# When the first gated weights are converted: behind the first attention results instead of ahead of them

## The chip, the cores and the metric

The kernel runs on one core of a Trainium2 chip. Its time is the device time of one execution in microseconds (us). Before the change three runs were timed; the median was 837.14 us, the lowest 832.61, the highest 839.86.

The engines work side by side, each in its own fixed order of instructions: TensorE (PE) multiplies, VectorE (DVE) and ScalarE (ACT) work on tiles, GpSimd (POOL) does a little and issues some transfers, SyncE (SP) issues most transfers. They wait for each other by semaphores. Matmul results land in PSUM, everything else is in SBUF or in DRAM.

## The reference

Three parts, one behind the other, all in fp32:

```python
scores = scale * q @ k.T;  scores = cap * tanh(scores / cap)        # 4 batches x 12 heads, 448 x 64
attn = softmax(scores) @ v                                          # scale = 1/8, cap = 30
x = attn, heads side by side                                        # 1792 tokens x 768
a, b = x @ w1, x @ w2;  h = (a * b) @ w3 @ w_out                    # 768 -> 1024 -> 1024 -> 768
h = h @ w_in                                                        # 768 -> 1024
solu = h * softmax(h);  ln = layer norm of solu, times g_ln
out = ln @ w_out2                                                   # 1024 -> 768
```

## The kernel before

**Arithmetic.** Each fp32 operand is split into a high and a low part that TensorE multiplies exactly, and a product is the sum of three matmuls (low times high, high times low, high times high; `THREE` lists which parts). The high part is a cast on ScalarE (L174), the low part a subtraction on VectorE (L175). Weights that come as fp32 words in a packed form are first brought into a work tile `cv` by three rows on VectorE (L168, L169, L170).

**Stages.** Attention runs over 24 pairs of heads (o12 is pair 12), each in four chunks (sc13_2 is the scores of chunk 2 of pair 13; p, hi and lo are its exponentials and their two parts; o13_0 and o13_1 its results, which ScalarE copies out of PSUM, L306). Beside it, with matmuls put between those of attention by `fill`, goes a second stream, `beside`: first the *fold*, which multiplies the weights w_out, w3 and w_in into one matrix, then the *gated* products x·w1 and x·w2 (L607). The fold has two stages: stage 1 makes the blocks w34 and stores them in DRAM (576 matmuls, L378), stage 2 loads them again, splits them, and multiplies by w_in (288 matmuls, L396, sixteen tiles f2_f_nh of eighteen each). `load34` has one block on its way while another is used. Behind attention come seven products for the second factor (L769), the layer norm and the last product.

**What sets the order.** `Ahead` holds a list of conversions that are taken strictly in turn, a few in each turn of the attention loop. An item has a load on SP into one of three landing tiles `ld`, a first step on VectorE, and a rest. The function given last with an item is its gate: while it says no, the item isn't loaded, nor is anything behind it. `pos[0]` counts the fold's matmuls as they are written, `STAGE1` is 576 and `HALFWAY` 144, so that `STAGE1 + HALFWAY` is the middle of stage 2.

The items that matter here: `plan_w(f)` converts block f of the gated weights in three items (512 KB loaded for each) into the tile wt*f*; wt0 and wt1 are the first two, wt0 is read first by the first gated matmul. `plan_x(b)` makes batch b's tokens xs from the attention results xr, in three parts; `free_x` is its gate. The numbers in ld40 or cv47 count the items of the list. In `gated`, each of the first six wt tiles is stored in DRAM for a second pass once the program comes to L618. `plan_last` scales the last weights by g_ln into one of two tiles wg (L539), which is stored in wg_dr (L540).

From these calls a scheduler makes each engine's order, so a change in the list can move rows on all engines.

Of the kernel before, what the change touches and what calls it, by code (L numbers as in the profile page):

```python
# [25 lines left out]
NC, NF = DM // P, DF // P  # L26
# [14 lines left out]
PASSES = ((0, 1), (2, 3))  # L41
# [4 lines left out]
def raw(ap):  # L46

    return ap.bitcast(F32)
# [50 lines left out]
def attention_moe_solu(ctx: ExitStack, tc: tile.TileContext, q, k, v, cap, w12, w3t, wo, win, wout2, g_ln, out):  # L99
# [50 lines left out]
    def landing(i, src, n, kind):  # L150
        t = conv.tile([P, 2 * HALF], U32, tag="ld", bufs=LANDS, name=f"ld{i}")
        lands[i] = t[:, :n].bitcast(kind)
        dst = lands[i]
        if len(src.shape) == 3:
            dst = dst.rearrange("p (a b) -> p a b", a=src.shape[1])
        elif len(src.shape) == 4:
            dst = dst.rearrange("p (a b c) -> p a b c", a=src.shape[1], b=src.shape[2])
            for g in range(src.shape[1]):
                sync.dma_start(out=dst[:, g], in_=src[:, g])
            return  # L160
        loads[i] = sync.dma_start(out=dst, in_=src)

    def convert(i, n):

        d = lands.pop(i).rearrange("p (n w) -> p n w", w=2)
        lo, hi = d[:, :, 0], d[:, :, 1]
        x = conv.tile([P, HALF], U32, tag="cv", bufs=2, name=f"cv{i}")[:, :n]
        dve.tensor_scalar(x, hi, 5, 2, ALU.logical_shift_left, ALU.logical_shift_right)  # L168
        dve.scalar_tensor_tensor(x, hi, 0xC0000000, x, ALU.bitwise_and, ALU.bitwise_or)  # L169
        dve.scalar_tensor_tensor(x, lo, 29, x, ALU.logical_shift_right, ALU.bitwise_or)  # L170
        cvs[i] = x.bitcast(F32)

    def split(th, tl, x):
        act.copy(th, x)  # L174
        dve.tensor_tensor(tl, x, raw(th), ALU.subtract)  # L175

    def plan64(key, src, n, dst, gate=None, there=None):

        i = len(ahead.items)

        def rest():
            th, tl = dst()
            split(th, tl, cvs.pop(i))
        ahead.add(key, lambda: landing(i, src.bitcast(U32), 2 * n, U32), lambda: convert(i, n), rest, gate, there)
# [139 lines left out]
    fw, pos, place, held = {}, [0], {}, {}  # L324
# [30 lines left out]
    STAGE1, HALFWAY = NQ * NC * NF * 3, NC * NF * 3  # L355
# [50 lines left out]
    wt, xs, rb, fin = {}, {}, {}, set()  # L406
# [5 lines left out]
    def slot12(f, i):  # L412
        if i == 0:
            p = place["wt"] if f >= NF and (f - NF) % 3 == 2 else res[0]
            wt[f] = p.tile([P, 2, 2 * DM], F32R, tag="wres", bufs=1 if p is not res[0] else 2, name=f"wt{f}")
        return wt[f][:, 0, i * HALF:(i + 1) * HALF], wt[f][:, 1, i * HALF:(i + 1) * HALF]

    def free12(f):

        if f == NF + 2:  # L420
            return "wt" in place
        before = f - 2 if f < NF + 2 else f - 3
        return pos[0] >= STAGE1 and (f < 2 or (before, PASSES[before // NF][-1]) in fin)

    def plan_w(f):
        for i in range(3):
            plan64(("w", f, i), w12[f, i], HALF, lambda i=i: slot12(f, i), lambda: free12(f))

    def plan_again(f):
        def load():  # L430
            for i in range(3):
                slot12(f, i)
            sync.dma_start(out=raw(wt[f]), in_=w12_dr[block(f)])
        for i in range(3):
            ahead.add(("w", f, i), load if i == 0 else (lambda: None), lambda: None, lambda: None, None, lambda: free12(f))

    def place_x(b, c):

        n = b * NC + c
        if n < W3 or n >= 2 * W3:  # L440
            return w3p.tile([P, 2, HALF], F32R, tag="w3", bufs=W3, name=f"xs{b}_{c}")[:, :, :S]
        return place["x"].tile([P, 2, S], F32R, tag="xs", bufs=W3, name=f"xs{b}_{c}")

    def free_x(b, part):
        if (b, part) not in stored:
            return False
        if b == 0:
            return pos[0] >= STAGE1 + (HALFWAY if part else 0)
        return (pos[0] >= STAGE1 + HALFWAY if (b, part) == (1, 0) else "x" in place) and (b < 3 or (NF - 1, 0) in fin)

    def plan_x(b, parts=range(NPAIR // 2)):
        for part in parts:
            if (b, part) == (B - 1, NPAIR // 2 - 1):

                plan_again(NF + 2)
            i = len(ahead.items)
            pairs = slice(2 * part, 2 * part + 2)

            def load(i=i, pairs=pairs):
                rb[i] = conv.tile([P, 2, S], F32, tag="rb", name=f"rb{i}")  # L460
                for j in range(2):
                    row = r_dr[b].rearrange("(n j) s -> j n s", j=2)[j:j + 1, pairs]
                    pool.dma_start(out=rb[i][j * D:(j + 1) * D], in_=row.to_broadcast([D, 2, S]))

            def first(i=i, part=part):

                for c in (2 * part, 2 * part + 1):
                    xs[b, c] = place_x(b, c)
                one = raw(xs[b, 2 * part + 1][:, 0, :1])
                pool.memset(one, 1.0)  # L470
                dve.scalar_tensor_tensor(xr[b, part], xr[b, part], one, rb.pop(i), ALU.mult, ALU.mult)

            def rest(part=part):
                x = xr.pop((b, part))
                for i in range(2):
                    split(xs[b, 2 * part + i][:, 0], xs[b, 2 * part + i][:, 1], x[:, i])
            ahead.add(("x", b, part), load, first, rest, None, lambda part=part: free_x(b, part))
# [55 lines left out]
    def plan_last(f):  # L533
        for u in range(2):
# [5 lines left out]
                sync.dma_start(out=wg_dr[f, u], in_=t)  # L540
            ahead.add(("g", f, u), lambda i=i, u=u: landing(i, wout2[f, u].bitcast(U32), DM, U32), lambda i=i: convert(i, DM // 2), rest)

    plan_w(0)
    plan_x(0)
    plan_w(1)
    plan_x(1)
    for f in range(2, NF):
# [419 lines left out]
```

## Time and profile before

| | before |
|---|---|
| runs | 837.14 us median (832.61, 837.14, 839.86) |
| the profiled execution's own time | 834.68 us |
| its span, first to last instruction | 832.9 us |
| mean granted TensorE clock | 0.998 |
| TensorE (PE) busy | 820.4 us, 98% |
| VectorE (DVE) busy | 586.8 us, 70% |
| ScalarE (ACT) busy | 478.8 us, 57% |
| GpSimd (POOL) busy | 75.8 us, 9% |
| moved by DMA | 167.19 MB, mean 201 GB/s |

Busy is the time in which an engine worked on an instruction, and the share is of the span. The granted clock is 1.00 where TensorE ran at 2.4 GHz all the time and 0.50 where at 1.2 GHz. Times in the rows further down count from the span's start.

### The profile page before, as it was taken

To read this page: it belongs to the slowest core of one execution; us is meant where nothing else is said; L and a number is where in the kernel's file an instruction comes from. 1 tells how busy PE (TensorE), PEld (TensorE's weight loads), DVE (VectorE), ACT (ScalarE), POOL (GpSimd) and SP (SyncE) were. 2 spreads that over 40 slices of the span, in tenths; PEclk is the share of its full clock that TensorE was granted. 3 is DMA by queue.
4 is the path that set the end of the run, shared out by engine and by line. 5 is a ranking of instruction groups with operands and counts; after the bars stand their busy time and mean duration, and the time that the engine had idled before them with its cause. 6 is when DMAs were issued, how large, how long until landed. Compare 5 with 4: busy or idle time off the path is not lost.

```text
span 832.9 us, 12192 instructions
## 1 busy us (share of the span) xinstructions
PE 820.4 (98%) x4363; PEld 683.6 (82%) x4363; DVE 586.8 (70%) x1048; ACT 478.8 (57%) x739; POOL 75.8 (9%) x149
## 2 busy tenths in 40 slices
PE   8999999999999999999989999999999999999998
PEld 4657888876777888888869999998888888999997
DVE  5989969788866797788826744332988876994452
ACT  6767868778777876777642301112565555863341
POOL 1110010110311211111111000000000000000000
PEclk9999999999999999999999999999999999999999
DMA  7888645568976465689537999972533326834211
GB/s 238 267 255 274 213 143 166 168 229 289 277 259 195 119 207 171 193 308 311 159 122 194 315 379 361 327 234 68 167 127 102 101 102 192 293 123 152 89 65 76
DMA packets 95069, 167.19 MB, mean 201 GB/s; under 512 B 13216, under 2 KB 66208, under 8 KB 93472
## 3 DMA queue, kind: packets, MB, share of 16 engines
q1 hardware_dynamic: 90016, 155.22, 55.7%
q0 software_dynamic: 4992, 11.19, 5.4%
q8 instruction: 34, 0.56, 0.3%
q14 instruction: 27, 0.22, 0.1%
HBM read 113.25 MB, written 47.53 MB: 193 GB/s over the span
## 4 chain that ended last, share of the span: by engine, by line
PE 81%; DMA 8%; DVE 7%; ACT 2%; issue 2%; SPq 0%; POOL 0%; DVEq 0%; ACTq 0%
PE ab L607 26%; PE u L769 16%; PE o L290 9%; PE v L769 8%; PE f L396 6%; PE f L378 5%; PE y L769 4%; PE sc L249 4%; DMA wg_dr<-wg 2%; PE tp L839 1%; DVE cv L169 1%; DMA ld<-in_wo 1%; DMA qd<-in_q 1%; DVE cv L170 1%; DMA ld<-in_w3t 1%
## 5 line engine op out<-in xcount | busy, mean ns | idle before, releaser
L607 PE MATMUL ab<-xs,wt 128*128 128x448 f32 x1152 | 242.2, 367 | 0.4 <-ACT x L306 0.4
L607 PEld LDWEIGHTS ab<-xs,wt 128*128 128x128 f32 x1152 | 216.4, 188 | 22.0 <-ACT x L306 0.8
L257 ACT ACTIVATE sc<-sc,qscale 128x896 f32<-128x896 f32 (+1 forms) x96 | 84.9, 884 | 38.0 <-PE sc L249 29.1
L290 PE MATMUL o<-hi,v 128*66 128x448 f32 (+1 forms) x360 | 86.1, 376 | 2.1 <-ACT x L306 2.0
L258 ACT ACTIVATE p<-sc,capt 128x896 f32<-128x896 f32 (+1 forms) x96 | 85.5, 916 | 1.4
L769 PE MATMUL u<-ws,a 128*128 128x512 f32 x336 | 81.5, 394 | 0.0
L378 PEld LDWEIGHTS f<-w,w_o 128*128 128x128 f32 x576 | 72.6, 191 | 10.7 <-issue 5.8
L378 PE MATMUL f<-w,w_o 128*128 128x256 f32 x576 | 78.3, 289 | 1.3 <-DVE w_o L175 0.9
L769 PEld LDWEIGHTS u<-ws,a 128*128 128x128 f32 x336 | 62.8, 187 | 14.7
L273 DVE TENSOR_TENSOR lo<-p,hi 128x896 fp32r<-128x896 f32 x60 | 65.0, 1084 | 13.9 <-ACT hi L269 13.5
L396 PE MATMUL f<-w_i,w 128*128 128x512 f32 x288 | 70.2, 393 | 1.1 <-ACT w L174 0.7
L396 PEld LDWEIGHTS f<-w_i,w 128*128 128x128 f32 x288 | 53.7, 188 | 14.5 <-issue 1.2
L769 PE MATMUL u<-wg,c 128*128 128x384 f32 x336 | 64.8, 340 | 0.0
L611 ACT COPY a<-ab 128x448 f32<-128x448 f32 x32 | 17.0, 531 | 82.2 <-PE ab L607 69.5
L290 PEld LDWEIGHTS o<-hi,v 128*66 128x66 f32 (+1 forms) x360 | 39.6, 136 | 27.9 <-issue 8.5
L769 PEld LDWEIGHTS u<-wg,c 128*128 128x128 f32 x336 | 58.3, 188 | 0.1
L269 ACT CAST hi<-p 128x896 fp32r<-128x896 f32 x60 | 56.6, 947 | 0.3
L615 DVE TENSOR_TENSOR abs<-ab,a 128x448 f32<-128x448 f32 x32 | 19.8, 620 | 50.4 <-PE ab L607 28.1
L169 DVE SCALAR_TENSOR_TENSOR cv<-ld,cv 128x512 uint32<-128x512 uint32 (+1 forms) x80 | 51.9, 657 | 0.6
L170 DVE SCALAR_TENSOR_TENSOR cv<-ld,cv 128x512 uint32<-128x512 uint32 (+1 forms) x80 | 52.0, 657 | 0.5
L168 DVE TENSOR_SCALAR cv<-ld 128x512 uint32<-128x512 uint32 (+1 forms) x80 | 32.5, 409 | 22.2 <-DMA ld<-in_w 7.7
L307 POOL DMA_DIRECT2D xr<-x x48 | 25.6, 538 | 202.2 <-ACT x L306 194.7
(132 smaller groups left out, 1253.1 us busy)
## 6 DMA issues: line engine op xcount, KB each, us to landing
ld<-in_w SPq DMA_DIRECT2D x24, 512.0 KB, 4.9
w_dr<-wt SPq DMA_DIRECT2D x6, 1536.0 KB, 6.9
wt<-w_dr SPq DMA_DIRECT2D x6, 1536.0 KB, 8.9
ld<-in_w3t SPq DMA_DIRECT2D x16, 512.0 KB, 4.7
ab_dr<-abs SPq DMA_DIRECT2D x32, 224.0 KB, 4.6
ldab<-ab_dr SPq DMA_DIRECT2D x14, 512.0 KB, 4.0
c_dr<-e SPq DMA_DIRECT2D x14, 512.0 KB, 2.7
ldc<-c_dr SPq DMA_DIRECT2D x14, 512.0 KB, 4.1
```

The source lines that it names most:

```text
L169: dve.scalar_tensor_tensor(x, hi, 0xC0000000, x, ALU.bitwise_and, ALU.bitwise_or)
L170: dve.scalar_tensor_tensor(x, lo, 29, x, ALU.logical_shift_right, ALU.bitwise_or)
L249: tiled[0] = pe.matmul(sc[:, j, :S], keys[rows], qq[rows, :], start=(m == 0), stop=(m == len(terms) - 1))
L257: act.activation(sc[:, :w, :S], sc[:, :w, :S], AF.Tanh, scale=qscale)
L258: exp_[n, c] = act.activation(p, sc[:, :w, :S], AF.Exp, scale=capt)
L269: act.copy(hi, p)
L273: dve.tensor_tensor(lo, p, raw(hi), ALU.subtract)
L290: product_.append(pe.matmul(outs[n, j][:v_.shape[-1], :S], v_, t[rows, j if c < 3 else 0], **flags))
L378: pe.matmul(f[:, :QW], lw[:, a], rw[:, e], start=(g == 0 and m == 0), stop=(g == NF - 1 and m == 2))
L396: pe.matmul(f, w34[:, a, c, :], rw[:, e], start=(c == 0 and m == 0), stop=(c == NC - 1 and m == 2))
L607: pe.matmul(pp[f, b, i][:, :S], w[:, u], xs[b, c][:, e], start=(c == 0 and m == 0), stop=(c == NC - 1 and m == 2))
L769: pe.matmul(bank, a[m][:, x, k * P:(k + 1) * P], wb[m][:, e, k, :], start=(first and k == 0 and i == 0), stop=(k == NF // 2 - 1 and i == 2 ...
```

## The change

The gate of the gated weights' blocks moves from the end of the fold's first stage to the middle of its second, and the first batch's tokens are put ahead of block 0 in the list. The list was w0, x0, w1, x1 and is x0, w0, w1, x1. Nothing else is edited; the numbers of w0's items change from 40 to 42 into 43 to 45.

```diff
--- before
+++ after
@@ free12
         before = f - 2 if f < NF + 2 else f - 3
-        return pos[0] >= STAGE1 and (f < 2 or (before, PASSES[before // NF][-1]) in fin)
+        return pos[0] >= STAGE1 + HALFWAY and (f < 2 or (before, PASSES[before // NF][-1]) in fin)
@@ the list
+    plan_x(0)
     plan_w(0)
-    plan_x(0)
     plan_w(1)
     plan_x(1)
```

The first place is SP's queue at the beginning of the fold's second stage (e2 are that stage's results on their way to DRAM, vd, qd and kd loads of attention). Before:

```order
L161 DMA ld34_3_0_2076<-w34_dr_57 128x768
L401 DMA w_dr_58<-e2_1_0_2073 128x512
L161 DMA ld40_2161<-in_w12 128x1024
L161 DMA ld41_2180<-in_w12 128x1024
L161 DMA ld42_2195<-in_w12 128x1024
L205 DMA vd12_2241<-in_v 128x448
L197 DMA qd13_2492<-in_q 128x448
L197 DMA kd13_2493<-in_k 128x512
L161 DMA ld34_4_0_2203<-w34_dr_57 128x768
L401 DMA w_dr_58<-e2_2_0_2200 128x512
```

Now:

```order
L161 DMA ld34_3_0_2076<-w34_dr_57 128x768
L401 DMA w_dr_58<-e2_1_0_2073 128x512
L161 DMA ld34_4_0_2200<-w34_dr_57 128x768
L161 DMA ld34_5_0_2243<-w34_dr_57 128x768
L161 DMA ld34_6_0_2338<-w34_dr_57 128x768
L205 DMA vd12_2238<-in_v 128x448
L197 DMA qd13_2467<-in_q 128x448
L197 DMA kd13_2468<-in_k 128x512
L401 DMA w_dr_58<-e2_2_0_2197 128x512
```

The three loads of block 0 are gone from there, and three loads of w34 stand in their place.

The second place is VectorE in the second half of stage 2, from the last step of v1 (pair 13's values) to the low half of w34_3_1. Before:

```order
L232 TENSOR_TENSOR v1_82<-vd13_2496,v1_82 128x7x64
L175 TENSOR_TENSOR w34_3_1_2759<-ld34_3_1_2757,w34_3_1_2759 128x768
L273 TENSOR_TENSOR lo12_2_2664<-p12_2_2660,hi12_2_2663 128x896
L175 TENSOR_TENSOR w34_4_1_2846<-ld34_4_1_2844,w34_4_1_2846 128x768
L272 CAST hi13_3_2698<-p13_3_2695 128x448
L273 TENSOR_TENSOR hi13_3_2698<-p13_3_2695,hi13_3_2698 128x448
L318 TENSOR_SCALAR inv1_4_2381<-inv1_4_2381,guard_72 112x16
L319 RECIPROCAL inv1_4_2381<-inv1_4_2381 112x16
L273 TENSOR_TENSOR lo13_0_2723<-p13_0_2719,hi13_0_2722 128x896
L231 CAST v0_81<-vd14_2608 128x7x64
```

Now the last twelve of the twenty rows behind that step of v1; the eight ahead of them are lo12_2, six rows of block 1's conversion, and the cast of hi13_3:

```order
L273 TENSOR_TENSOR hi13_3_2673<-p13_3_2670,hi13_3_2673 128x448
L318 TENSOR_SCALAR inv1_4_2366<-inv1_4_2366,guard_72 112x16
L169 SCALAR_TENSOR_TENSOR cv48_2815<-ld48_2708,cv48_2815 128x512
L231 CAST v0_81<-vd14_2583 128x7x64
L175 TENSOR_TENSOR wt1_2806<-cv47_2809,wt1_2806 128x512
L319 RECIPROCAL inv1_4_2366<-inv1_4_2366 112x16
L170 SCALAR_TENSOR_TENSOR cv48_2815<-ld48_2708,cv48_2815 128x512
L232 TENSOR_TENSOR v0_81<-vd14_2583,v0_81 128x7x64
L273 TENSOR_TENSOR lo13_0_2699<-p13_0_2695,hi13_0_2698 128x896
L218 CAST qh15_2987<-qd15_2876 128x448
L218 CAST kh15_2991<-kd15_2877 128x512
L175 TENSOR_TENSOR w34_3_1_2740<-ld34_3_1_2738,w34_3_1_2740 128x768
```

The low half of w34_3_1 stood right behind v1 and now stands twenty rows behind it, behind both steps of v0 too. On TensorE the rows of f2_3_1 stand right behind o12; now the scores sc13_1 and sc13_2, and ten matmuls of o13 stand between. On SP, the load vd14 that v0 reads now stands right behind wt0's store (before, right behind wt1's).

The third place is ScalarE near the end of attention (the wg rows are `plan_last`, a_5_0 is a gated product). Before:

```order
L539 ACTIVATE wg5_0_4822<-cv77_4794,gt_74 128x384
L257 ACTIVATE sc23_3_4545<-sc23_3_4545,qscale_71 128x448
L258 ACTIVATE p23_3_4549<-sc23_3_4545,capt_70 128x448
L258 ACTIVATE p23_0_4555<-sc23_0_4499,capt_70 128x896
L539 ACTIVATE wg5_1_4831<-cv78_4825,gt_74 128x384
L269 CAST hi23_0_4558<-p23_0_4555 128x896
L306 COPY x22_4597<-o22_0_4506 65x448
L306 COPY x22_4597<-o22_1_4507 65x448
L611 COPY a_5_1_4765<-ab0_5_1_4711 128x448
```

Now:

```order
L258 ACTIVATE p23_0_4555<-sc23_0_4499,capt_70 128x896
L539 ACTIVATE wg4_1_4791<-cv76_4785,gt_74 128x384
L539 ACTIVATE wg5_0_4822<-cv77_4794,gt_74 128x384
L269 CAST hi23_0_4558<-p23_0_4555 128x896
L306 COPY x22_4597<-o22_0_4506 65x448
L306 COPY x22_4597<-o22_1_4507 65x448
L611 COPY a_5_0_4686<-ab0_5_0_4580 128x448
L539 ACTIVATE wg5_1_4831<-cv78_4825,gt_74 128x384
```

wg5_1 stood ahead of hi23_0 and of the copies of x22 and now stands behind them; wg4_1 and wg5_0 stand later than before.

## Rows read from the trace of the kernel before

**Rows 1.** The page's first part: busy us (share of the span) xinstructions.

```profile
PE 820.4 (98%) x4363; PEld 683.6 (82%) x4363; DVE 586.8 (70%) x1048; ACT 478.8 (57%) x739; POOL 75.8 (9%) x149
```

**Rows 2.** Windows: us, then busy time by engine, clock, DMA share, GB/s.

```profile
core 0: us, PE busy (x) PEld busy (x) DVE busy (x) ACT busy (x) POOL busy (x), PEclk, DMA share, GB/s
190.00:200.00 10.00, 8.40 (x42) 6.13 (x42) 10.00 (x18) 9.12 (x13) 0.00 (x0) 1.00 0.74 248
200.00:412.00 212.00, 212.00 (x1123) 169.20 (x1122) 162.83 (x279) 156.88 (x224) 33.76 (x67) 1.00 0.70 225
420.00:425.00 5.00, 4.58 (x16) 2.77 (x17) 2.00 (x4) 4.97 (x8) 1.58 (x3) 0.66 0.67 187
433.00:825.00 392.00, 392.00 (x1970) 352.40 (x1971) 243.79 (x449) 160.10 (x277) 16.59 (x25) 1.00 0.54 183
```

**Rows 3.** TensorE's timeline at 190 us: start, us, row, [idle before <-releaser].

```profile
191.09 0.47 PE L249 MATMUL sc<-ql,kh 64*128 64x448 f32 x2 [0.52 <-ACT p L258]
...
193.26 0.73 PE L396 MATMUL f<-w_i,w 128*128 128x512 f32 x2 [0.67 <-ACT w L174]
194.41 0.96 PE L396 MATMUL f<-w_i,w 128*128 128x512 f32 x3 [0.41 <-DVE w L175]
```

**Rows 4.** TensorE's timeline, 412 to 433 us.

```profile
413.06 0.62 PE L290 MATMUL o<-lo,v 128*66 128x448 f32 x2 [0.53 <-DVE lo L273]
...
420.41 2.60 PE L290 MATMUL o<-hi,v 64*66 64x448 f32 x8 [2.04 <-ACT x L306]
...
432.93 1.29 PE L607 MATMUL ab<-xs,wt 128*128 128x448 f32 x5 [0.41 <-ACT x L306]
```

**Rows 5.** ScalarE's timeline, 418 to 421 us.

```profile
418.49 0.61 ACT L539 ACTIVATE wg<-cv,gt 128x384 f32<-128x384 f32 x1 [3.73 <-DMA wg_dr<-wg]
419.01 0.92 ACT L269 CAST hi<-p 128x896 fp32r<-128x896 f32 x1
419.83 0.95 ACT L306 COPY x<-o 65x448 f32<-65x448 f32 x2
```

**Rows 6.** Groups by line: xcount | busy us, mean ns of one | idle before, releaser.

```profile
L170 DVE SCALAR_TENSOR_TENSOR cv<-ld,cv 128x512 uint32<-128x512 uint32 (+1 forms) x80 | 52.0, 657 | 0.5
L169 DVE SCALAR_TENSOR_TENSOR cv<-ld,cv 128x512 uint32<-128x512 uint32 (+1 forms) x80 | 51.9, 657 | 0.6
L168 DVE TENSOR_SCALAR cv<-ld 128x512 uint32<-128x512 uint32 (+1 forms) x80 | 32.5, 409 | 22.2 <-DMA ld<-in_w 7.7 <-DMA ld<-in_wo 4.8 <-DMA ld<-in_win 2.7
...
L175 DVE TENSOR_TENSOR wt<-cv,wt 128x512 fp32r<-128x512 f32 x24 | 15.9, 677 | 0.7 <-ACT wt L174 0.7
```

**Rows 7.** DMA issues of the page: xcount, KB each, us to landing.

```profile
w_dr<-wt SPq DMA_DIRECT2D x6, 1536.0 KB, 6.9
```

**Rows 8.** Windows around w1's conversion, columns as in the other windows.

```profile
217.00:227.00 10.00, 10.00 (x52) 6.71 (x49) 8.78 (x16) 7.48 (x12) 3.01 (x5) 1.00 1.02 285
227.00:237.00 10.00, 10.00 (x50) 7.18 (x49) 9.55 (x17) 9.27 (x15) 1.90 (x4) 1.00 0.96 323
```

**Rows 9.** VectorE's timeline, 231 to 241 us.

```profile
231.58 0.62 DVE L232 TENSOR_TENSOR v<-vd,v 128x448 fp32r<-128x448 f32 x1
232.11 0.95 DVE L175 TENSOR_TENSOR w<-ld,w 128x768 fp32r<-128x768 f32 x1
...
240.24 0.62 DVE L231 CAST v<-vd 128x448 fp32r<-128x448 f32 x1 [2.40 <-DMA vd<-in_v]
```

**Rows 10.** TensorE's timeline, 226 to 243 us.

```profile
226.67 5.20 PE L396 MATMUL f<-w_i,w 128*128 128x512 f32 x22
231.79 0.83 PE L290 MATMUL o<-hi,v 64*66 64x448 f32 x6
...
236.92 3.12 PE L396 MATMUL f<-w_i,w 128*128 128x512 f32 x13
...
241.30 1.33 PE L290 MATMUL o<-hi,v 64*66 64x448 f32 x8
```

**Rows 11.** SP's issues, 231 to 233 us.

```profile
231.69 0.32 SPq L618 DMA_DIRECT2D w_dr<-wt  x1
232.22 0.33 SPq L205 DMA_DIRECT2D vd<-in_v  x1
```

**Rows 12.** The tile vd: landing times of its twenty loads.

```profile
DMA to landing us min/median/max: 2.5/3.5/7.9
```

**Rows 13.** TensorE's timeline at the first gated matmul.

```profile
271.97 0.78 PE L607 MATMUL ab<-xs,wt 128*128 128x448 f32 x3
```

## The prediction

> **What bounds the kernel now.** I read the page's first part first: TensorE is busy for 820.4 of 832.9 us [rows 1], so a change that does the same work in another order can win only the few microseconds in which TensorE waits, and can lose by making new waits. The work is the same here: the same conversions, loads and stores, by the order of the instructions. Next I read the stretches of the span from 190 us on, where the first of the moved rows stand, for TensorE's idle time: from 200 to 412 us it is busy for all 212.00, from 433 to 825 for all 392.00 [rows 2]. Two places are left, and TensorE's timeline shows each.
>
> Place A lies at 190 to 195 us: TensorE sits idle for 0.52 us behind ScalarE's exponentials, 0.67 us for the cast of w34_4_0 and 0.41 us for its low half on VectorE [rows 3], 1.6 us in all. The stretch around it shows why: VectorE is busy for the whole 10.00 us and ScalarE for 9.12, TensorE for 8.40 [rows 2]. That is where w0 is loaded and converted, and its three loads stand on SP's queue ahead of the load of w34_4_0.
>
> Place C lies at 412 to 433 us. TensorE waits 0.53 us for a low half of the probabilities, 2.04 us at 420.41 for ScalarE's copies of an attention result out of PSUM, and 0.41 us once more [rows 4]. ScalarE was late there because it had stood 3.73 us in wg5_1, which waited for a buffer whose store to wg_dr had not landed; the cast of hi23_0 and the two copies are queued behind it [rows 5]. In the five microseconds from 420 the granted clock is 0.66 on average, between the two levels of 1.2 and 2.4 GHz, where it is 1.00 around place A, whose longest idle is 0.67 us [rows 2, 3]. At 0.66 five microseconds do the work of 3.3, so the clock took 1.7 us more. Place C cost 0.53 + 2.04 + 0.41 + 1.7 = 4.7 us.
>
> **The gate and the swap.** The three items of w0 now wait until the middle of the fold's second stage and stand behind x0's three. w1, whose place in the list was already behind x0's second part with that same gate, is not moved in the list, but it meets w0 in the same stretch of time.
>
> *Removed at place A.* On SP the loads ld40 to ld42 are gone from ahead of w34_4_0's load. On VectorE twelve rows go: for each of three items 0.409 + 0.657 + 0.657 + 0.677 = 2.40 us, 7.2 us together [rows 6]; on ScalarE three casts of the same tiles, 1.9 us at the same length. On the DMA engines three loads of 128x1024 elements, 512 KB each, and the store of wt0, 1536 KB [rows 7], leave that stretch. VectorE had no idle time there and loses 7.2 us of work, and w34_4_0 can be loaded and split ahead of need. I take the whole 1.6 us as gone: -1.6. Bounds: 0, if the exponentials and w34_4_0 are late for another reason, to -1.6, all there is.
>
> *Added at 211 to 245 us.* The same 7.2 us of VectorE, 1.9 us of ScalarE, and 3 MB of traffic. From 217 to 237 us VectorE is busy for 8.78 and 9.55 of every 10 us already, with w1's conversion in it, and the DMA engines are full (1.02 and 0.96) [rows 8]. So VectorE cannot take both in that stretch, and by the order of its instructions part of w1's conversion moves behind v1<-vd13, between it and the low half of w34_3_1. That half is what the third matmul of f2_3_1 needs. Call this place B.
>
> Before, the last step of v1 ends at 231.58 + 0.62 = 232.20 us (call this D), the split follows at once and ends at 233.06 [rows 9]; f2_3_1 starts at 236.92 [rows 10], 3.9 us later, so nothing waits. Now twenty rows run from D to the end of the split. The 33 rows of 217 to 237 us took 8.78 + 9.55 = 18.33 us [rows 8], 0.555 each: 11.1 us, so it is ready at D + 11.1. TensorE ends f2_2_1 at 231.87, D - 0.3 [rows 10]. Between it and the third matmul of f2_3_1 stand now: 5.1 us as before (231.79 to 236.92), then the scores sc13_1 and sc13_2, which took 241.30 - 240.04 = 1.3, eight matmuls of o13 at 1.33 and two more, 0.4, and two matmuls of f2_3_1, 0.5 [rows 10]. It comes there at D + 8.3 and waits 11.1 - 8.3 = 2.8 us.
>
> Two things come on top. The cast v0<-vd14 is one of the twenty rows. Its load was issued at 232.22, half a microsecond behind wt1's store of 1536 KB [rows 11], and VectorE stood 2.40 us idle for it at 240.24 [rows 9], with no harm, as nothing urgent was behind it. Now it stands right behind wt0's store instead, and w34_3_1 is behind its cast. Such loads land in 2.5 to 7.9 us [rows 12]. VectorE comes to the cast after eleven rows, some 6 us behind D; whether the load is there by then depends on when SP reaches it. From below this costs 0, from above the same 2.40; I take the middle, 1.2, as the landing times spread over both sides of 6 us. And a wait of about 3 us may cost clock as the 2.04 us of place C did: 0 to 1.7. The waits here would be cut into pieces, as two of place A's are, so I take half, 0.8. Together place B costs 2.8 + 1.2 + 0.8 = 4.8 us. Bounds: 0, if TensorE finds other rows or VectorE catches up, to 8.9, the whole conversion of 7.2 us on the path and 1.7 of clock.
>
> On the store the Trainium skill, "DMA: Bandwidth & Descriptors", section "Issuing engines are not separate DMA queues", speaks against the change: it says that transfers started by any engine end up on the same 16 DMA engines and interleave there, so that a second queue only saves issue time. By it vd14 shares the engines with wt0's store whatever queue either is on, and takes its longest landing; the waits then would be the 2.40 and the 1.7 whole, and the sum -1.6 - 4.7 + 2.8 + 2.4 + 1.7 = +0.6 instead of -1.5. The trace agrees as far as the share of 0.96 to 1.02 goes, and the long landings; which of the loads it falls on is not shown.
>
> *Cover that is lost.* The first gated matmul, the first reader of wt0, is at 271.97 us [rows 13]. By the order wt0's store now stands where wt1's stood, at some 232 us [rows 11], so wt0 is ready by then, 40 us ahead; wt1 follows twelve such rows of VectorE later. This costs nothing. If the cover were gone, gated matmuls would wait 2.4 us per item.
>
> *Place C.* It is moved by the order alone: the gated work between is dealt out differently from 240 us on, so that on ScalarE hi23_0, both copies x22 and one a_5_0 now stand ahead of wg5_1. The copies no longer wait for the store. All of the 4.7 us can go (bound -4.7), or none (0) if wg5_0, which still stands ahead, waits in place of wg5_1 (its buffer was last stored by wg4_0, one step earlier). I take the whole, since the store that was waited for belongs to the row that has gone behind.
>
> **Sum.** -1.6 - 4.7 + 4.8 = -1.5 us on the profiled execution's 834.68, that is 833.2. The median of the runs shown, 837.14, stands 2.5 us above the profiled one, and the three spread from 832.61 to 839.86; against the median the forecast is 837.14 - 1.5 = 835.6.
>
> **Rivals.**
> 1. *VectorE's backlog decides, and the change is slower.* Place B is paid near its upper bound (the split waits for vd14 behind wt0's store, and the clock falls), 7.0 to 8.9, and wg5_0 takes over the wait at C. For it: the full DMA share, and 2.40 us of VectorE idle for that very load. Against: ScalarE's order at C. Price: -1.6 + 7.0 = +5.4, 842.5 us, at most +7.3, 844.4; it decides once place B costs more than 1.6 with C's wait kept, or 6.3 without. Chance 0.25.
> 2. *Both old waits go and B is hidden.* TensorE's rows slide, w34_3_1 comes in time: -6.3, 830.8 us. For it: 3.9 us of slack at f2_3_1 before, and the 1.2 us that VectorE is idle from 217 to 227 us [rows 8]. Against: the count of twenty rows. Chance 0.22.
> 3. *The waits only change places, and nothing is gained:* 837.1 us. A stays for the exponentials, C for wg5_0, B is short. Chance 0.10. That the change does nothing is excluded, as hundreds of rows stand elsewhere on each engine.
>
> The forecast itself has 0.43; its own range is 833 to 839 (B between 2 and 8).
>
> **How the numbers follow.** 829 is the second rival less 2 us for the spread of the runs' median, 844 the first rival's upper price. Outside lie lower times (0.05) and new waits beyond the first rival or a high median (0.13). About 1%, 8.4 us, is what a measurement of this kernel can tell from no change: faster means under 828.8, slower over 845.5. Under 828.8 there is nothing in TensorE's idle time to win, only the runs' own spread: 0.04. Over 845.5 would take place B's upper bound and a new wait beyond, in the gated part: 0.09. The rest, 0.87, is within.
>
> **What would show it.** Right: no wait at w34_4_0; TensorE waiting 2 to 5 us at o13<-lo13_0 or f2_3_1 with VectorE as the releaser, and VectorE on w1's rows ahead; no 3.73 us of ScalarE at wg. Wrong: new waits in the gated part, where I assume none; ScalarE late at wg5_0; a clock below 1.00 for more than a few microseconds; or f2_3_1 starting with no wait at all.

## The result and the profile after

| | before | after |
|---|---|---|
| median of 22 runs each | 834.22 us (832.01 to 839.86) | 838.99 us (836.35 to 844.27) |
| ratio after/before | | 1.0065, 95% interval 1.005 to 1.0079 |
| profiled execution, own time | 834.68 us | 839.95 us |
| span | 832.9 us | 838.1 us |
| mean granted TensorE clock | 0.998 | 0.995 |

The change makes the kernel slower by 0.65%; a gain of 1.5 us was forecast. TensorE does the same work (4363 matmuls) and is busy for 822.2 us instead of 820.4 [rows 1], so of the 5.2 us of span 3.4 are idle time of TensorE, and the rest is longer work, which the clock below tells of. Of the idle time 0.9 us lie ahead of 190 us, where TensorE's rows still stand in the old order (the first two windows, before and after), so the change did not make them. The other windows are those of the kernel after, with the columns of [rows 2]:

```profile
core 0: us, PE busy (x) PEld busy (x) DVE busy (x) ACT busy (x) POOL busy (x), PEclk, DMA share, GB/s
0.00:190.00 190.00, 186.18 (x1130) 139.22 (x1130) 159.26 (x288) 140.27 (x209) 23.85 (x54) 1.00 0.69 217
0.00:190.00 190.00, 185.32 (x1125) 139.52 (x1126) 158.13 (x284) 142.32 (x211) 23.78 (x54) 1.00 0.69 214
190.00:200.00 10.00, 10.00 (x51) 7.71 (x50) 7.07 (x12) 6.88 (x10) 0.00 (x0) 1.00 0.67 219
235.00:240.00 5.00, 2.38 (x13) 1.68 (x13) 4.96 (x11) 4.16 (x7) 0.27 (x1) 0.88 0.98 349
240.00:245.00 5.00, 4.34 (x21) 2.44 (x18) 4.95 (x10) 3.65 (x6) 1.85 (x4) 0.78 0.80 258
305.00:310.00 5.00, 2.38 (x13) 1.60 (x12) 2.47 (x3) 1.28 (x3) 0.00 (x0) 1.00 0.40 83
310.00:315.00 5.00, 5.00 (x19) 4.53 (x18) 5.00 (x11) 4.93 (x9) 0.45 (x1) 0.66 0.12 46
420.00:425.00 5.00, 3.80 (x25) 2.08 (x22) 3.09 (x6) 1.81 (x5) 1.59 (x3) 1.00 0.92 305
433.00:825.00 392.00, 392.00 (x1972) 353.06 (x1971) 243.83 (x448) 160.95 (x277) 16.51 (x25) 1.00 0.53 183
```

Place A is gone: TensorE is busy for 10.00 of the 10 us that it worked 8.40 in before. Two stretches that had no idle time before [rows 2, second row] now have a wait of 2.62 us each, and around and behind them the clock is below 1.00 (0.88 and 0.78, and 0.66). TensorE's timeline names what they wait for:

```profile
238.56 0.54 PE L249 MATMUL sc<-ql,kh 64*128 64x448 f32 x2 [2.62 <-ACT p L258]
...
243.82 0.72 PE L396 MATMUL f<-w_i,w 128*128 128x512 f32 x2 [0.66 <-ACT w L174]
...
309.74 0.62 PE L290 MATMUL o<-lo,v 128*66 128x448 f32 x2 [2.62 <-DVE lo L273]
...
424.44 0.42 PE L290 MATMUL o<-lo,v 128*66 128x448 f32 x1 [1.20 <-DVE lo L273]
```

The first is place B, the scores sc13_1. ScalarE's timeline ahead of it:

```profile
235.81 0.62 ACT L174 CAST wt<-cv 128x512 fp32r<-128x512 f32 x1 [3.24 <-DVE cv L170]
236.34 0.60 ACT L257 ACTIVATE sc<-sc,qscale 128x448 f32<-128x448 f32 x1
236.97 1.53 ACT L258 ACTIVATE p<-sc,capt 128x448 f32<-128x448 f32 x2
```

ScalarE stood 3.24 us in the first cast of wt1, for words that VectorE had not made, and the exponentials of sc13_3 and sc13_0 stood behind it. TensorE waited for the tile of PSUM that they free. VectorE had itself been idle for a load ten microseconds earlier:

```profile
226.03 0.43 DVE L168 TENSOR_SCALAR cv<-ld 128x512 uint32<-128x512 uint32 x1 [2.13 <-DMA ld<-in_w]
...
239.65 0.62 DVE L231 CAST v<-vd 128x448 fp32r<-128x448 f32 x1
```

That was w0's third item (ld45, issued at 218.07 us, some 8 us before). The second row is v0<-vd14: it didn't wait, where it stood 2.40 us before [rows 9].

The smaller wait, 0.66 us, is for the cast of w34_3_1, whose own load came late too. It was issued behind wt0's store at 235.81 us, where it was issued at 225.04 before:

```profile
242.93 0.83 ACT L174 CAST w<-ld 128x768 fp32r<-128x768 f32 x1 [1.35 <-DMA ld<-w_dr]
```

The wait at 309.74, call it place D, lies in the gated part. VectorE's timeline there (xr2_1 scales tokens of batch 2 by their row sums, which come back from DRAM as rb87; the second row is lo16_2):

```profile
307.53 1.15 DVE L471 SCALAR_TENSOR_TENSOR xr<-xr,xs,rb 128x896 f32<-128x896 f32 x1 [5.20 <-DMA rb<-r_dr]
308.60 1.08 DVE L273 TENSOR_TENSOR lo<-p,hi 128x896 fp32r<-128x896 f32 x1
```

In the kernel before, the same two rows stood in this order at 301 us with a wait of 0.77 us; twelve rows of VectorE lay between xr2_1 and the reciprocal of those sums, where seven lie now, and the sums came back 6.4 us behind the issue of their load instead of 4.6.

Place C shrank to the 1.20 us at 424.44: wg5_1 still waits for its store (3.19 us), but now with the copies of x22 ahead of it, and the clock stays at 1.00 where it was 0.66 [rows 2]. The 1.20 us are for a low half on VectorE, which had stood 1.86 us for another load of weights.

**Corrections to the text above.** The kernel's description says that an item's gate holds its load and all behind it. That holds for the tokens' items, whose function `free_x` is given last (`there`). The weights' `free12` is given one place earlier (`gate`), and `step` asks it only ahead of the first VectorE row. So it doesn't hold the load. The first experiment shows what that does to the change. The packed weights are 64-bit words, not fp32 words: an item of 128x512 values is 512 KB, and the three rows of VectorE make one fp32 word out of the two halves of each. That TensorE multiplies the two parts exactly is shown by no run here; nothing below rests on it.

### The profile page after: what moved, and what is told of

Same layout as the page of the kernel before. It is cut to its first block, busy times and chain, and to the rows that moved or that the text cites. A ratio compares the mean times of both kernels' runs of the same rounds, so it can differ in the third digit from the quotient of the medians.

```text
span 838.1 us, 12201 instructions
## 1 busy us (share of the span) xinstructions
PE 822.2 (98%) x4363; PEld 685.6 (82%) x4363; DVE 586.3 (70%) x1048; ACT 480.2 (57%) x739; POOL 75.6 (9%) x149
## 4 chain that ended last, share of the span: by engine, by line
PE 70%; DVE 12%; DMA 11%; issue 3%; ACT 2%; POOL 0%; SPq 0%; DVEq 0%; POOLq 0%; ACTq 0%
PE ab L607 22%; PE u L769 16%; PE v L769 8%; PE o L290 5%; PE f L396 5%; PE f L378 4%; PE y L769 4%; DMA ld<-in_w 3%; PE sc L249 3%; DVE cv L169 3%; DVE cv L170 2%; PE tp L839 1%; DVE cv L168 1%; DMA ld<-in_wo 1%; DVE lo L273 1%
## 5 line engine op out<-in xcount | busy, mean ns | idle before, releaser
L170 DVE SCALAR_TENSOR_TENSOR cv<-ld,cv 128x512 uint32<-128x512 uint32 (+1 forms) x80 | 52.3, 661 | 0.6
L169 DVE SCALAR_TENSOR_TENSOR cv<-ld,cv 128x512 uint32<-128x512 uint32 (+1 forms) x80 | 51.7, 661 | 0.6
L290 PE MATMUL o<-lo,v 128*66 128x448 f32 x120 | 42.3, 366 | 3.8 <-DVE lo L273 3.8
```

The lines of the kernel that those rows point to most:

```text
L290: product_.append(pe.matmul(outs[n, j][:v_.shape[-1], :S], v_, t[rows, j if c < 3 else 0], **flags))
```

## The experiments

Each run's time stands against runs of the kernel before that were taken beside it on the same chip. Profiled executions are single ones, so a wait is read from a profile and a time from the medians.

**Which of the two edits acts.** The list's new order alone gives the same program as the whole change, instruction for instruction, so it wasn't run apart. The gate alone:

```diff
-        return pos[0] >= STAGE1 and (f < 2 or ...
+        return pos[0] >= STAGE1 + HALFWAY and (f < 2 or ...
```

> The first line of the change alone: the gate of the gated weights moves to the middle of the fold's second stage, the list stays w0, x0, w1, x1. Theory L (what counts is when w0's loads are issued; this gate holds only the first conversion step in the program's text, not the load, and the scheduler puts every row where it was before): 834.2 us as before, within 1 us, with the waits of place A (about 190 to 195 us) and place C (about 420 us) both there. Rival G (the gate carries the change): 839 us or a good part of the way there.

834.91 us against 834.28, ratio 1.0004 (0.9989 to 1.0018). Apart from the numbers of tiles, its rows on all engines are those of the kernel before. The gate does nothing; the whole change is the order of the list.

As these are the rows of the kernel before, the run also tells how far two executions of one program differ at place C:

```profile
415.24 0.62 PE L290 MATMUL o<-lo,v 128*66 128x448 f32 x2 [1.30 <-DVE lo L273]
421.77 1.59 PE L290 MATMUL o<-hi,v 64*66 64x448 f32 x7 [1.24 <-ACT x L306]
420.00:425.00 5.00, 3.75 (x22) 2.26 (x19) 2.73 (x4) 4.97 (x8) 1.59 (x3) 1.00 0.86 270
```

The long wait of 2.04 us is here two of 1.30 and 1.24, and the clock is 1.00 where it was 0.66 [rows 2, 4].

**Is it x0 ahead, or w0's loads late?** Here w0's items get a function that holds the load, with the list as it was:

```diff
-            plan64(("w", f, i), ..., lambda: free12(f))
+            plan64(("w", f, i), ..., lambda: free12(f), (lambda: pos[0] >= STAGE1 + 144) if f == 0 else None)
```

> Before, with the list unchanged (w0, x0, w1, x1), but w0's loads themselves held until the middle of the second stage. TensorE's order of rows is then that of the changed kernel, though x0 is not ahead of w0. Theory L (the late loads are the change): 838 to 840 us, with the two new waits of about 2.6 us on TensorE at the scores sc13_1 (236 us) and at o16<-lo16_2 (307 us). Rival O (that x0 comes ahead is what costs): 834 us and neither wait.

839.78 us against 834.28, ratio 1.0068 (1.0044 to 1.0092). TensorE's rows are those of the changed kernel, in the same order, with both new waits:

```profile
239.49 0.47 PE L249 MATMUL sc<-ql,kh 64*128 64x448 f32 x2 [2.62 <-ACT p L258]
...
309.85 0.62 PE L290 MATMUL o<-lo,v 128*66 128x448 f32 x2 [1.85 <-DVE lo L273]
```

So holding w0's loads does what the change does, and x0's place ahead of w0 isn't needed for it. Place D is smaller here than in the changed kernel (1.85 us and 0.65 at 317.50) and the clock behind it stays at 1.00. x0's later parts hold the loads of all that stands behind them until the middle of stage 2, and w0 now stands behind them. The same edit with 96 and 120 in place of 144:

> Before, with w0's loads held until the 96th of the 288 matmuls of the second stage, a third of the way. w0's conversion then falls between place A and w1's conversion, and TensorE's order is that of before but for 48 rows. Theory L: A's 2.3 us go, no wait at sc13_1 nor at o16<-lo16_2, C stays: 831.5 to 833.5 us. Rival (any later w0 makes VectorE late further on): 836 to 839 us.

> Before, with w0's loads held until the 120th of the 288 matmuls, between the run at 96 and the middle. Theory L, with VectorE's backlog growing as w0's loads come nearer to w1's: A gone, C there, and a short wait of up to 2 us about sc13_1: 832 to 835 us. Rival (a threshold, only the middle and later cost): 831.5 to 833.5 us as with 96.

96: 837.99 us, ratio 1.0058 (1.0035 to 1.008). 120: 835.23, ratio 1.0005 (0.9989 to 1.0021). Place A is gone in both, but at 96 TensorE waits 2.01 us at 205.80 for a cast of w34 and 2.35 at 239.51 for exponentials, at 120 1.62 us at 223.37; place C stays in both, and place D is in neither. My number for 96 was wrong: there was no free place between A and w1.

**Do the two queues make the waits, or pass them on?** On the changed kernel, wt1's first cast goes behind p13_0 on ScalarE:

```diff
-            split(th, tl, cvs.pop(i))
+            with tc.issue_after(exp_[13, 0].ins) if key == ("w", 1, 0) else nullcontext(): split(th, tl, cvs.pop(i))
```

> The changed kernel, with ScalarE's first cast of wt1 put behind the exponentials p13_0 (before them it stood waiting 3.24 us for VectorE, with them queued behind it). Theory S (TensorE's wait at sc13_1 comes through ScalarE's queue: the cast waits for VectorE's late conversion, and the exponentials that free the scores' bank wait behind it): the 2.62 us wait and the slower clock behind it go, 4 to 5 us less: 834 to 835.5 us. Rival V (VectorE is late there anyway, and TensorE meets it a few rows later at o13<-lo13_0 or at w34_3_1): 837.5 to 839 us, the wait only moves.

839.47 us against 832.94, ratio 1.0083 (1.006 to 1.0105). The rival was right in kind; the wait moved one step on, behind VectorE's low half of wt1:

```profile
239.72 2.33 PE L290 MATMUL o<-hi,v 64*66 64x448 f32 x10 [1.73 <-DVE wt L175]
242.90 1.01 PE L290 MATMUL o<-lo,v 128*66 128x448 f32 x2 [0.85 <-DVE lo L273]
```

xr2_1 behind lo16_2 on VectorE (place D):

```diff
-                dve.scalar_tensor_tensor(xr[b, part], ...)
+                with tc.issue_after(exp_[16, 2, 1].ins) if (b, part) == (2, 1) else nullcontext(): dve.scalar_tensor_tensor(xr[b, part], ...)
```

> The changed kernel, with VectorE's scaling of xr2_1 put behind the low half lo16_2 (ahead of it it stood waiting 5.20 us for the row sums from DRAM, rb87, with lo16_2 queued behind it). The rows behind are dealt out anew. Theory Q (that one row ahead of lo16_2 is place D): the 2.62 us at o16<-lo16_2 and the slower clock behind it go, 3 to 4 us less: 835 to 836 us. Rival (VectorE is late there for want of time): another wait of 2 us or more comes within 20 us, 838 to 839.5 us.

840.32 us, ratio 1.0091 (1.0066 to 1.0115). No wait at lo16_2 is left, though VectorE stood 3.69 us at xr2_1 then, with nothing urgent behind. But the rows behind were dealt out anew, and place C was back, ScalarE first and then TensorE:

```profile
427.47 0.62 ACT L539 ACTIVATE wg<-cv,gt 128x384 f32<-128x384 f32 x1 [2.90 <-DMA wg_dr<-wg]
```

```profile
422.92 0.62 PE L290 MATMUL o<-lo,v 128*66 128x448 f32 x2 [1.17 <-DVE lo L273]
429.39 1.81 PE L290 MATMUL o<-hi,v 64*66 64x448 f32 x8 [1.14 <-ACT x L306]
```

Both moves at once:

> The changed kernel with both rows put behind: ScalarE's cast of wt1 behind p13_0, and VectorE's xr2_1 behind lo16_2. If the two new waits are the whole cost and the two old ones (places A and C) are gone in the main, 4.5 + 3.5 us less than 839.0: 830.5 to 832 us, faster than the kernel before. Rival (the late w0 costs by other ways too): 834 us or more.

843.33 us, ratio 1.0126 (1.01 to 1.0151): by the median slower than either, though the intervals still touch.

**Place C by itself**, on the kernel before, where `exp_[22, 9]` is the second copy of x22:

```diff
-                act.activation(t, cvs.pop(i), AF.Copy, scale=gt[:, f:f + 1])
+                with tc.issue_after(exp_[22, 9].ins) if (f, u) == (5, 1) else nullcontext(): act.activation(t, ...)
```

> The kernel before, with one row of ScalarE moved: wg5_1 behind the two copies of x22, so that neither hi23_0 nor the copies wait for the store to DRAM (one row of VectorE moves with it, TensorE's order is the same). Theory C (that wait of 2.04 us and the clock behind it are worth what place C was priced at): 829.5 to 831 us. Rival (the gated products behind wait instead, for ScalarE's later copies): 833.5 to 834.5 us.

830.96 us against 832.94, ratio 0.9975 (0.9963 to 0.9986): faster than both kernels by moving one row. The place's window, which had 18.0 us of TensorE's work before (21 us less the three waits of [rows 4]):

```profile
412.00:433.00 21.00, 20.59 (x109) 16.99 (x108) 10.12 (x18) 12.68 (x20) 3.14 (x6) 1.00 0.48 155
```

In the profile, of the place's waits only 0.41 us are left, and the clock is 1.00 throughout. The medians differ by 2.0 us, less than half of the 4.7 that the place was priced at. The clock is the likely reason: the 17 runs of the kernel before that stand beside this one have a mean clock of 0.999, where the profiled one has 0.998, so on the whole they lost less time to the clock. The waits that went, 0.53 and 2.04, are 2.6 us.

**VectorE's time, or late loads?** First the changed kernel with less VectorE work (for w0 the rows L169 and L170 are left out):

```diff
-        dve.scalar_tensor_tensor(x, hi, 0xC0000000, x, ...)
-        dve.scalar_tensor_tensor(x, lo, 29, x, ...)
+        if i not in (43, 44, 45): dve.scalar_tensor_tensor(x, hi, 0xC0000000, x, ...)
+        if i not in (43, 44, 45): dve.scalar_tensor_tensor(x, lo, 29, x, ...)
```

> The changed kernel, with two of VectorE's three rows that make w0's words left out (six rows of 0.66 us, 3.9 us; wt0 then holds other values). Its loads, casts, stores and their times on the DMA engines stay. The rows around are dealt out anew. Theory V (place B is want of VectorE time: w0 and w1 in the same stretch): no wait of over 1 us on TensorE from 200 to 260 us, 833 to 835.5 us. Rival M (place B is late loads on full DMA engines): waits of some 3 us in that stretch stay, 837 to 839 us.

838.21 us against 833.75, ratio 1.0049 (1.0033 to 1.0065). The waits of place B stayed: with 3.9 us less to do VectorE waits for w1's load, ScalarE for VectorE, TensorE for ScalarE. One row of each engine:

```profile
225.81 0.43 DVE L168 TENSOR_SCALAR cv<-ld 128x512 uint32<-128x512 uint32 x1 [1.65 <-DMA ld<-in_w]
```

```profile
228.20 0.62 ACT L174 CAST wt<-cv 128x512 fp32r<-128x512 f32 x1 [3.50 <-DVE cv L170]
```

```profile
233.28 0.47 PE L245 MATMUL sc<-ql,kh 128*128 128x448 f32 x1 [2.24 <-ACT p L258]
```

The time itself tells less: some 300 of TensorE's rows stand elsewhere than in the changed kernel, place D is gone, and place C is back with a wait of 1.99 us.

w1 out of w0's way, by a function that holds w1's loads until `STAGE1 + 228`:

```diff
+            plan64(..., lambda: free12(f), (lambda: pos[0] >= STAGE1 + 228) if f == 1 else None)
```

> The changed kernel, with w1's loads (and all that stands behind them in the list) held until the 228th of the 288 matmuls of the fold's second stage, so that w0 and w1 are not converted in the same stretch. Theory V (w0 and w1 together are too much for VectorE from 211 to 245 us): the waits there go, 4 to 5 us less, 833 to 835.5 us, if the later w1 makes no new wait. Rival (each stretch of attention is full for VectorE, and wherever a block's conversion comes late, TensorE waits by its length): a wait of 2 us or more between 245 and 300 us, 837 to 840 us.

848.84 us, ratio 1.0167 (1.0147 to 1.0186), the slowest of all. No wait of 2.6 us at 236 any more, but as large and larger ones later, among them for w34's low half and for the gated products' results:

```profile
268.10 5.08 PE L396 MATMUL f<-w_i,w 128*128 128x512 f32 x14 [4.07 <-DVE w L175]
...
385.35 1.91 PE L607 MATMUL ab<-xs,wt 128*128 128x448 f32 x8 [2.81 <-DVE abs L615]
```

The run with xr2_1 moved, with wg5_1 moved as well:

> The changed kernel with xr2_1 behind lo16_2, as in the run before this one, and wg5_1 behind the copies of x22 on ScalarE, as in the run on the kernel before. In the first of these wg5_1 was back ahead of the copies and waited 2.90 us for its store. If place D's gain was given back by that row: 2 to 4 us under the run with xr2_1 moved alone, so 836 to 838 us. Rival (the profile's single wait isn't what the median is made of): 839.5 to 840.5 us.

839.40 us against 833.75, ratio 1.0055 (1.0034 to 1.0075). TensorE's wait for the copies of x22 is gone in the profile. Against the run without wg5_1 moved it is 0.9 us by the medians and 3 us by the ratios, each taken against other runs of before, and the two intervals overlap. Inconclusive.

Then the changed kernel with two loads of w0 left out; the second and third item use the landing tile of the first:

```diff
-        ahead.add(key, lambda: landing(i, ...), ...)
+        ahead.add(key, (lambda: lands.__setitem__(i, lands[i - 1])) if key in (("w", 0, 1), ("w", 0, 2)) else lambda: landing(i, ...), ...)
```

> The changed kernel, with the loads of w0's second and third item left out (1 MB less on the DMA engines; their words are made from the first item's, so wt0 holds other values). All of VectorE's and ScalarE's rows stay, and TensorE's order but for 28 rows. Theory M (place B begins with loads that land late: six of 512 KB in a row on full DMA engines, VectorE idle for them, ScalarE's casts of wt1 late behind, the exponentials queued behind those): the waits of over 1 us from 225 to 250 us go, 834 to 836 us, place D being left. Rival V (VectorE's and ScalarE's work itself is too much there): a wait of 2 us or more stays, 838 to 840 us.

832.71 us against 835.14, ratio 0.9976 (0.9962 to 0.9991). No wait of 0.3 us or more is left between 200 and 300 us, and place D is down to 1.36 and 0.66 us. TensorE's order is that of the changed kernel but for a few rows, so the new order by itself is not what costs. VectorE's work in the stretch is the same, and it is now busier than in the changed kernel (10.00 us against 7.84). The windows are the changed kernel's first, then two of the run without the loads:

```profile
220.00:230.00 10.00, 10.00 (x47) 6.86 (x46) 7.84 (x16) 5.50 (x9) 0.63 (x2) 1.00 1.02 283
220.00:230.00 10.00, 10.00 (x47) 6.83 (x46) 10.00 (x18) 7.08 (x12) 2.18 (x5) 1.00 0.90 264
230.00:240.00 10.00, 10.00 (x54) 6.24 (x54) 9.52 (x19) 9.41 (x15) 2.14 (x4) 1.00 0.93 324
```

So VectorE can do the work of w0 and w1 in that stretch, if the words are there. The view of the landing tiles from 208 to 236 us shows why they are not: in the kernel before (nine loads, three of them of 512 KB), in the changed one (seven, six of 512 KB), and without the two loads (six, four of 512 KB),

```profile
DMA to landing us min/median/max: 3.7/4.7/8.4
```

```profile
DMA to landing us min/median/max: 3.2/7.1/9.1
```

```profile
DMA to landing us min/median/max: 3.3/3.8/6.3
```

wt0's store is not what made them late: in the changed kernel it was issued at 232.72 us, behind all six, and it stays in this run. What it costs the load of w34_3_1 was not tried.

**The order on the queues, once more in full.** All of wt1's casts behind p13_0 and its low halves behind lo13_0 (the `with` of the first cast, with both anchors, for all three items); then with xr2_1 and wg5_1 moved too:

> The changed kernel, with all of wt1's casts on ScalarE behind p13_0 and all its low halves on VectorE behind lo13_0, so that no row of wt1's last step stands ahead of what pair 13's scores and results wait for. In the run with the first cast alone moved, TensorE's wait went over to o13<-hi13_0, behind VectorE's low half of wt1. Theory S (the order on the two queues passes the lateness on, row by row): waits from 225 to 250 us of 1 us in all or less, 834.5 to 836 us. Rival V (the conversion's other rows, on VectorE ahead of the attention's, are late enough by themselves): 2 us or more of waits stay there, 838 to 840 us.

> The same with xr2_1 behind lo16_2 and wg5_1 behind the copies of x22 too: every row that was found with TensorE waiting behind it is moved. If the four places add up, 839.0 less 4.5 (B), 3 (D) and 1 (what is left of C): 830 to 832 us. Rival (each move opens a wait elsewhere, as the moves one by one did): 836 to 839 us.

840.48 us, ratio 1.007 (1.0048 to 1.0092), and 840.82, ratio 1.0074 (1.0048 to 1.01). The rivals were right in kind both times, and both times came out above the rivals' ranges. In the first, TensorE's waits from 237 to 244 us were four of 0.8 to 1.3 us, the last two for w34's casts, and place D stayed (2.39 us):

```profile
242.52 0.73 PE L396 MATMUL f<-w_i,w 128*128 128x512 f32 x2 [1.33 <-ACT w L174]
244.15 7.20 PE L396 MATMUL f<-w_i,w 128*128 128x512 f32 x18 [0.90 <-ACT w L174]
```

**One or two loads late instead of three**, by splitting w0's items in the list (`plan_w` takes which):

```diff
-    plan_w(0)
-    plan_x(0)
+    plan_w(0, (0, 1))            # one early: (0,)
+    plan_x(0); plan_w(0, (2,))   # (1, 2)
```

> The kernel before, with w0's first two items where they were and the third behind x0, so that one of w0's loads comes among w1's instead of three. Theory M (place B is made by the loads of w0 and w1 in a row, and grows with their number): little or nothing at 225 to 250 us, A shorter by some part, 832 to 835 us, the three copies in C still behind wg. Rival (any part of w0 that late makes the wait): 837 to 839 us.

> The kernel before, with w0's first item where it was and two behind x0, so that two of w0's loads come among w1's. Theory M: between the run with one and the changed kernel: waits of 1 to 3 us at 225 to 250 us, 834 to 838 us. Rival (what counts is how the rows are dealt out, not the number of loads): no order among the three.

> The run with one of w0's loads late, and wg5_1 behind the copies of x22 as well. If both gains hold: 829 to 831.5 us, faster than either kernel. If the loads among w1's cost as in the changed kernel: 833 to 836 us.

841.63 us, ratio 1.0078 (1.0058 to 1.0097); 841.61, ratio 1.0082 (1.0058 to 1.0105); 839.70, ratio 1.0068 (1.0048 to 1.0088). None of the three times came out in a range that was forecast for it. Place B alone follows the number of loads: with one late TensorE waits 0.50 and 0.26 us there, with two 1.82 and 0.30, with three 2.62 and 0.66. The time does not: new waits stand elsewhere, with one late load the largest at 395 us, where ScalarE had stood 4.16 us in a wg for its store, ahead of the copies of x, as at place C:

```profile
395.10 0.64 PE L290 MATMUL o<-hi,v 64*66 64x448 f32 x1 [3.61 <-ACT x L306]
```

**The two old waits without late loads**: the kernel before, with wg5_1 moved as above and VectorE's low half of w0's second item behind that of w34_4_0 (`issue_after`, as above):

> The kernel before with wg5_1 behind the copies of x22 on ScalarE, and on VectorE the low half of wt0's second item behind that of w34_4_0, for which TensorE waited 0.41 us in the kernel before and 0.72 us in the run with wg5_1 moved. TensorE's order stays that of the kernel before. If both old waits can be taken away without late loads: 0.4 to 0.7 us under the run with wg5_1 alone, and 2 to 4 us under the kernel before, 830 to 831.5 us against 833 to 835. Rival (the order there is worth nothing, as the load of w34_4_0 is late): as with wg5_1 alone.

832.15 us against 835.75, ratio 0.996 (0.9943 to 0.9976). Faster than both kernels; its interval overlaps that of wg5_1 alone, so the second row isn't shown to add anything. In its profile TensorE still waited 0.86 us for the cast of w34_4_0.

## Why the prediction was wrong

- **Place A, -1.6.** Right. The wait at w34_4_0 is gone, and so is that for the exponentials.
- **The gate.** Wrong as told: w0's items are held by x0's parts in the list, not by their own gate, which changes no row. That it was the list didn't alter the sum.
- **Place B, +4.8.** The size holds by luck, as its parts don't. TensorE waited 2.62 + 0.66 = 3.3 us (2.8 taken). The clock of 0.88 and 0.78 in two windows of 5 us took 0.6 + 1.1 = 1.7 us (0.8 taken, 1.7 was the bound). vd14 cost nothing (1.2 taken). The count of VectorE's rows held: the low half of w34_3_1 ended 10.9 us behind v1's last step (11.1 taken), and TensorE, late by then, used it at 244.81 without a further wait. The wait came one place ahead of that, through ScalarE's queue, and the runs put it on late loads (with two fewer it goes) rather than on VectorE's work. I took the rows' data to be there, and of the moved step's own loads I counted only what they take from others.
- **On the Trainium skill's rule** ("DMA: Bandwidth & Descriptors", section "Issuing engines are not separate DMA queues"): the traces agree that transfers share the engines: in the changed kernel 1.02 of their time is used from 220 to 230 us, and the landing tiles' median goes from 4.7 to 7.1 us. I hung it on vd14, which it did not hit; it hit w0's and w1's own loads.
- **Place C, -4.7.** Mostly right: 1.20 us of wait is left, at another row and at full clock, so -3.5. That it was a real cost is shown by moving wg5_1 alone; that it was worth 4.7 isn't. The median gained 2.0 us there, and the same rows in the gate's run had no clock below 1.00. I had priced one execution.
- **"New waits in the gated part, where I assume none."** This is the step that failed: a term that the sum put at nothing. Place D took 2.62 us and five microseconds at a clock of 0.66, 1.7 us more: +4.3 in this profile. (With the same rows in the run that holds the loads it was 2.5 us of waits and no clock.) Without this term the sum would be -0.1. Nothing in the prediction followed the rows of the order past 245 us on VectorE, though the order showed xr2_1 right ahead of lo16_2, with seven rows between it and the reciprocal instead of twelve.

By these places the sum is -1.6 - 3.5 + 5.0 + 4.3 = +4.2. With the 0.9 us ahead of 190 us that is 5.1, against 5.2 us between the two spans; the medians differ by 4.8. The first rival had the sign and the whole clock, but its two prices were not what came: B stayed under its 7.0 us, and C did not wait on at wg5_0. That 838.99 lies between the forecast's bounds of 829 and 844 is in part luck: they stand around the 837.14 of three runs, 2.9 us above the median of 22. From 834.22 the forecast would be 832.7, and the kernel came out 6.3 us above it.

What stays open: taking D away (no wait left there) or moving the rows of places B, C and D at once did not bring the time down. Each of those edits dealt out some 200 rows of TensorE anew. With xr2_1 moved, the profile tells where D's time went: TensorE is busy 1.2 us less than in the changed kernel (821.0 us) but idle for 2.3 us more. Between 250 and 400 us it is idle for 1.3 less, but at place C for 1.5 more, from 190 to 250 us for 0.9 more, and in the first 100 us, where no row has moved, for 1.4 more. Profiles are single executions, though, and that the medians are made up alike isn't shown. So place D is shown as a wait and by the row that makes it, but what it is worth by itself is not.

## What to carry to other kernels

Follow a moved load to its own landing: how many others of its size are issued around it, whether the DMA engines are full there, and what is queued on each engine behind the row that waits for it; a row that waits passes its lateness on to whatever an in-order queue has behind it, and moving that row away can hand it to the next, as it did here with wt1's cast. Where a scheduler deals out the program, read the new order on every engine to the end of the stretch that it touches, not only up to the place that the edit names. A price read from one profile holds for one execution: the clock above all differed between executions of the same rows. And look for the row to move alone: here one row of one engine, with TensorE's order left as it was, gave 2.0 us, more than the 1.5 that were forecast for the change.

## What was not expected of the hardware

With the DMA engines' share at 1.02 (220 to 230 us), a load of 512 KB, 4.9 us by the median of the kernel before, took about 8 us (ld45); in the run with one late load the 384 KB of w34_3_1, issued behind wt0's store, took 11.4 us. In the changed kernel the granted clock fell behind each wait of 2.62 us of TensorE (0.78 and 0.66 in the five microseconds after) and stayed at 1.00 around the one of 1.20 us. The length of a wait alone doesn't tell it: the clock also stayed at 1.00 behind 2.35 us in the run at 96 (239.51 us), and behind 2.81 and 2.65 us in the run with w1 later (385.35 and 412.36 us).
